# One slot for the values' sums, bf16 filler matmuls of 512 columns, and a new issue order in a sketched-attention and experts kernel

## The chip, the cores and the metric

The kernel runs on one core of a Trainium2 chip, in one launch. Times are device microseconds (us). The core's engines work side by side, each through its own list in order: PE does the matmuls (PEld is its loading of the stationary operand), DVE, ACT and POOL work on vectors, and SP issues most DMAs. In this kernel PE's results go to PSUM, from where DVE and ACT read them. A matmul of f32 operands shows in the trace as two weight loads and two matmul records; a transpose on PE shows as one of each.

## The reference

Two parts follow each other, for a batch of 4, 1088 positions and 4 heads of 32:

```
phi(x) = (S1 x) outer (S2 x)            # 8 x 8 features per position and head
kv = sum_s phi(k) v ;  z = sum_s phi(k)
x  = (phi(q) kv) / (phi(q) z + 1e-6)    # heads side by side: (4, 1088, 128)

logits = x w_gate ; the two largest of 4 experts, softmax weights over these two
for each expert e:  a = softmax(causal(scale (x wq_e)(x wk_e)^T))
                    out += weight_e * (a (x wv_e)) wo_e     # where e was chosen
```

## The kernel before

**Stages.** For each of the four batches b the kernel first makes x (`prepare`, L342): the sketches of k and q (`sketch`, L434), ACT copies of these (L444), features on DVE or POOL (L454), the sums kv (L489), transposed features (L503), numerators (L524), the division on DVE (L532 to L535), x transposed (L541) and the logits (L585). From the logits DVE chooses the experts (`choose`, L608 to L615). Positions are cut into 17 pieces of 64, and these into groups 0, 1 and 2 of 6, 6 and 5 pieces. For each group come the queries (`queries`, matmuls L707, picked by masks on DVE at L717), the scores of each piece (`scores`: matmul L749, DVE takes them at L754, exponential on ACT at L769, reciprocal on DVE at L774, scaling on POOL at L778, transpose on DVE at L783), the values' sums (`values`, L805), the reading of these sums (two copies by ACT at L829, two products at L839 and two predicated copies at L843 on DVE) and the output product (`outputs`, L863).

**PSUM.** Four single tiles `bank0` to `bank3` serve most matmuls (pool `ps`). One further tile, `V`, spans four banks (L137). Before the main work, batch 0 uses three of V's banks as slots of the pool `ps0` (L143), one bank each, for its sketches, sums, transposes, logits and masks. Later V holds the values' sums: a group writes columns 0 to 191 of all four banks, or columns 256 to 447, the two slots of the pool `V` (L144). The framework that builds the program makes an instruction wait for earlier accesses of the list that it takes to be in conflict with it.

**Batch 0's masks.** The masks of its group 0 do not go through memory: six products of a one-hot matrix with the choice (`widen_masks`, L636) spread them over the partitions, each into a slot of `ps0`, and ACT or DVE copies each out (L641). The query picks at L717 need these copies.

**Order.** The kernel collects 1320 jobs, each with its engine, the values that it reads, what it makes and the slots that it holds. `ORDER` (L68) is a list of job numbers, two letters each, written out beforehand; `Plan.run` (L34) issues the jobs in that order and hands a slot to the first job that names it and back after the last. So the list fixes each engine's order and also which access of a PSUM tile counts as the earlier one. The entry `--` is no job but calls `nothing` (L926): a matmul of zeros into the last 64 columns of V's fourth bank, which nobody reads. The list has 69 of them, all before the first values' sums. They stand in runs, called filler matmuls here: 39 before the first sketch, then 1, 10, 2, 1, 1, 3, 5, 1 and 6.

Decoded, PE's list up to the first scores runs as follows (sk: sketch of k or q, batch/half; kv: sums; tq: transposed features; wt, mp: products of weights; num, tx, lg: numerators, transposed x, logits of a third; qe: queries; sc: scores; a number times `--` is a run of filler matmuls):

```
39x-- sk/k/0/1 -- sk/k/0/0 10x-- sk/q/0/0 kv kv tq/1 tq/0 wt0 wt1 2x-- sk/q/0/1 -- mp/1 sk/k/1/0
num/0 sk/k/1/1 tq/2 tq/4 tx/0 -- tq/3 num/1 sk/q/1/1 sk/q/1/0 tx/1 num/2 lg/1 3x-- tx/2 mp/0 lg/2 lg/0
4 qe 5x-- 3 masks -- 3 masks 6x-- 3 tq of batch 1, qe, 3 sc, tq, sc, qe, kv of batch 1, qe, kv of batch 1, ...
```

Where the sums of two groups meet, PE's list has this many other PE jobs between the last block of the one group and the first of the next (batch,group): 0,0 to 0,1: 20; to 0,2: 14; to 1,0: 11; to 1,1: 16; to 1,2: 0; to 2,0: 41; to 2,1: 0; to 2,2: 20; to 3,1: 0; to 3,2: 3; to 3,0: 0. At the five with 0 or 3, some of the reads of the earlier group (L829, L839, L843) stand in the list after the first blocks of the next.

Of the kernel before, what the change touches and what calls it, by code (L numbers as in the profile page):

```python
# [10 lines left out]
BF16 = mybir.dt.bfloat16  # L11
# [7 lines left out]
class Plan:  # L19
# [10 lines left out]
    def job(self, eng, us, rank, f, reads=(), makes=None, holds=(), kb=0.0, wait=0.0):  # L30
        self.jobs.append(dict(eng=eng, us=us, rank=rank, f=f, reads=tuple(reads), makes=makes, holds=tuple(holds),
                              kb=kb, wait=wait, n=len(self.jobs)))
# [34 lines left out]


ORDER = """
AAACAEABADATASAUAQARAFAPAVAWALANAMAIAJAOAGAHAKAbAZ------------------------------------------------------------------  # L70
------------AhAjAi--AdAkAfAeAgAaAXFlAc--------------------AlAYAmAvFmAnAoAwA0FpAxAyFoA1B6FnAzB8FrB7FqB9----ApAqAr--CB
FsAuAsFuFwCDCCA8FxAtFyF2A9FzA2F4F3F0A6BAA+A3A7Ft--A4F1A/FvBFA5F5GDBGF9F6GFGEBHBJF/BOF8BIGGF+BZBPGABa------BQBSGIB+BR
BEBBBbGCB/BDCABXBcBMBvCGGHBKBLCJCHBNF7CIBCBYCEBwBdBWB1CFBxGBB2BT----------BkBiBqBVBeBlGJBjBzBf--BmBoB3BrBgBUBpBnBhCL
C2C7CK------------GRCNGNGSCMGVGODMBsB4GWCOCaCPCsCQCbGTCcCRCtCgGUCdDJChCuB5BtGLBuDKCvCSByCiCeCTDHCwCjCfGKDICkCxB0ClGM
DLDNEJEEDOCmDPEVDQEXEWCnKoDXEcEYKqCoEbDlKrDYDnKmDmDZCUCpEZDoCqCVDpEaDaEdKsDbGPCrKpCWEeDtKnDcGQDvCXDuGpCYDqDwDrEfCZDx
GqCyDyDsGtDzGgEgD0CzGhD1GrD2C0GkGsKvG2C1GiC9C6DRC3G3GjC+G0C4C8DdG1DfC5D3DeDSDBD4DTKwC/D5DUDgDVDAKuDhDWGXD6KtDCD7EpFT
DEGYFYDGEhDFDDD8GZGbEnGaEiGyDiEjEoDjFBGzEqFDEkE/ErDkElHHG4D9HID+EsFAG5EmEtD/G+FCG6HAEuEAHBG8HCFEFFEBECG/FGLEG7EGEIED
FHELE3G9LGEHLFExEMEKE4EvFIEFE5LHEwPnE6HFLJEyE7EOPoHLLKHDHKLIHGE8EPEzHME9HOKxE0IKE1KyE+KzIIILK0INE2IJENHEK1IOFJIPH3K2
EQIRH8K3ETESJYEUPuK5ERIMK4PwJZK6JWIQJaJXK8JcIYJdJeISK7IZI4ITIaK9IeLMIUIbIfIcIVK+IdIWLLPxK/LAIXLBHJPqLNPvPrJbLDHNPpI2
JfPtLCHnPsI3HVHoFKI5HpHWLSI6HqLUHrLWFLLTI7I8LVIgHXGfFMGeI9LXGcGdIhFNHYIiHZHhIjFOIkHiHjIlFPGoGmHkHlGlHPFQGnHQHRFRHSHT  # L80
LQGwHmFSPyGuFXFaFULRGvHaJwHUGxPzFbFZP0HsHtJxP1HbHuKCP3HcHvKAFVFWHdJyP2HwKBFcHeKDHxJzFeHfHyJ0HgFdFgJ1J2HzKZKUFfH0FjFk
FiH1FhIuH+H2H7JgH5H4IvIwH6H9JiIxH/KEIyJ3IAIBIzKFI0JhKGIoJjImI1JkICKHInKIIpJ6JKJlJFJ4JmKJIqLOIDJ5LPJoIEIrIHJ7IsLqIFJp
J8IGJqItLrI+J9JrLuJ+LsJnLhJsI/J/LtLiLYJAJtLlLZJuLjLcJvLaLkL3LbL1L4LzL2MGL0L5NJMHMLNKMIJBMJMBL6MCJCMDL7JDL9KKJHJEL/JJ
JMKLJIJNJGMEKML8MFJLL+KNLfMALeKOLdLgKPKQLpLmMMLoKRMNLnMPJPNLJONQNMNPMKNNMOJQNRMiOGMQOLMjNOMRJRKSMSJTNSOZLxMkMTKbMUNT
LvKWKYLwKcKTNZLyKaOaMVNUJSJVN3KVKXNVJUNaOXNWKdNbMlN4NXOdMmOYKfNYNcMnNdP4OeKhNeMuP5P6MWMvKeP7MXMwNnP9KgMxP/M9KlNoM4Kj
OcMyQAKkNpMYOgKiP+N5MzQBP8NqNvN6NrNxQCMZNwQMNyN7MaNsQEMbMoNzN8QNQDMpMqN0N1QFQOMrQPMsN2QGObQHNtQQQRMtMcOfQIQSNfNuQZN9
MdNgMeOhQaQKOjOiQbQdQLNhN+QcQJQ0OkPFQ1OlQXNiQVMfPBMgQYOmMhQWOnPDPCNjOxPEPGQTOyPHOzNkNlM0O0QUPINmPJO1QrQiQsM1QjQvQtOp
QuO2QmO3Q4OqQkOrQ5QlQ2OsRJQ3OtQ6M2N/RKM3M8M5OAPKQ7RCOoQ+OBM+RDRAO4REOCQ8M/M6ODOuM7NAOEQ/OvRBRFNCOIOFOKONQ9OHNDOJOOOM
NBOwRGO5PaPVSXNEO6NFRHSYNIO7NHRNRINGRORMO8SVRQO9OQSbORSWO+O/ScRLTnPATlToOPRPTmTrRXTsSESJRvOSRYRnOVRZOWRROTOURaRtRSRb
PLRuRTRcRlRwR1RURxRmRVPMRoR2RpRyRWPNRzRqRrRdR0QhRfQfReQgSZRsQeSaRgR3SdRhPOSeR4RiR5SfRjShSgS3RkSiS5R6SjS4R7PPS6SkS7R8  # L90
PQSlSvQqS8S9QpSxQnSwQoS/SyTBTASzTDTCTpTES0PRTFTtS1PSTGTHPTR9QwSmPZQzPUPbQxS+QyR+PWPcS2SnR/PdPXTISpSAPYSoSqPeSrSBSCSs
StPfSLSDSISuSFPgPhSKSMTqPiSGUcPkTJUXSHPjPmTuPlSOUHUNUISPUJUOUPUKSNULUQUMTvURSQT7TwTKTTSUUSTxSRT8STTYTyUBTzT9SST1TLT0
UCT2UDT+T/TMT3UEUAUFT4TNT5UGT6TOTPTQTRUTTVTSTXTaTUTWUUTbTZUVTcUZUbUWUeUdTdUaUfUYTeTfUhTgTkThUgTjTiUiUjUkUlUmUn
"""


# [1 line left out]
def kernel(  # L98
# [14 lines left out]
    nc = tc.nc  # L113
# [17 lines left out]
    def const(name, shape, dt=F32):  # L131
        return cp.tile(shape, dt, name=name, tag=name)

    def several(name, n, shape, dt=F32):
        return [const(f"{name}{x}", shape, dt) for x in range(n)]

    V = pp.tile([128, 4, 512], F32, tag="V", name="V")  # L137
    banks = [pp.tile([128, 512], F32, tag=f"bank{x}", name=f"bank{x}") for x in range(4)]
# [2 lines left out]
    pools = dict(  # L141
        ps=banks,
        ps0=[V[:, x] for x in range(3)],  # L143
        V=[V[:, :, 0:192], V[:, :, 256:448]],  # L144
        kin=several("kin", 1, [128, S]),
        qin=several("qin", 1, [128, S]),
        vp=several("vp", 1, [128, NJ, H, D + 1]),
# [16 lines left out]
        A=several("A", 4, [128, S]),  # L164
# [13 lines left out]

    idle = const("idle", [128, 128])
    SKW = const("SKW", [128, 2, 2, 2, R])
    ident = const("ident", [128, 128])
    mask = const("mask", [128, 512], BF16)
# [608 lines left out]
    def values(b, n, rank):  # L793
        t0, t1 = groups[n]
        nt = t1 - t0
        AT, Vk, agg, mb = ("AT", b, n), ("V", b, n), ("agg", b, n), ("mb", b, n)
        J = 2 * t1

        def block(j0, j1):
            a = plan[AT][:, 0 : J * nt * 32].rearrange("p (j t s) -> p j (t s)", t=nt, s=32)  # L800
            for j in range(j0, j1):
                lo = 32 * max(0, j // 2 - t0)
                for g in range(4):
                    rows = slice(32 * g, 32 * g + 32)
                    nc.tensor.matmul(plan[Vk][:, g, lo : 32 * nt], plan[(f"xr{j // 12}", b)][rows, j % 12], a[rows, j, lo:],  # L805
                                     start=(j == 0), stop=(j == J - 1))

        def cost(j0, j1):
            n = [32 * (nt - max(0, j // 2 - t0)) for j in range(j0, j1)]
            return sum(max(0.22, 2 * x / 1200 + (0.03 if x > 160 else 0.006)) for x in n)  # L810

        for j0 in range(0, J, 4):
            j1 = min(j0 + 4, J)
            xr = (f"xr{j0 // 12}", b)
            need = [("AT", b, n), ("xr", b, j0 // 12)] + before
            before[:] = [("V", b, n, j0)] if j1 < J else [("V", b, n)]
            job("PE", cost(j0, j1), rank + 0.001 * j0, lambda j0=j0, j1=j1: block(j0, j1), need, before[0], [AT, Vk, xr])
# [10 lines left out]
        def keep(x):  # L828
            nc.scalar.copy(halves(plan[uw][:, x, 0:w]), part(x))  # L829

        def widen(x):
            nc.scalar.copy(plan[agg][:, 3 * x, 0:w], plan[mb][:, 3 * x, 0:w])

        def outer(x):
            a = plan[agg][:, 3 * x, 0:w]
            nc.gpsimd.tensor_tensor(out=a, in0=a, in1=plan[uw][:, x, 0:w], op=ALU.mult)  # L836

        def inner(x):
            nc.vector.tensor_tensor(out=halves(plan[agg][:, 1 + x, 0:w]), in0=part(x),  # L839
                                    in1=halves(plan[mb][:, 1 + x, 0:w]), op=ALU.mult)  # L840

        def patch(x):
            nc.vector.copy_predicated(halves(plan[agg][:, 1 + x, 0:w]), halves(plan[mb][:, E + x, 0:w]), part(1 - x))  # L843

        r = rank + 0.1
        for x in range(2):
            job("ACT", w * 0.00084 + 0.05, r, lambda x=x: keep(x), [("V", b, n)], ("uw", b, n, x), [Vk, uw])
            job("ACT", w * 0.00094 + 0.05, r - 0.05, lambda x=x: widen(x), [("mb", b, n)], ("agw", b, n, x), [agg, mb])
            job("POOL", w * 0.0023 + 0.08, r, lambda x=x: outer(x), [("uw", b, n, x), ("agw", b, n, x)], ("agg", b, n), [uw, agg, mb])
            job("DVE", w * 0.00104 + 0.08, r, lambda x=x: inner(x), [("V", b, n)], ("agg0", b, n, x), [Vk, agg, mb])  # L850
            job("DVE", w * 0.00104 + 0.08, r, lambda x=x: patch(x), [("agg0", b, n, x)], ("agg", b, n), [Vk, agg, mb])
# [72 lines left out]
        if b + 1 < B:  # L924
            prepare(b + 1, lambda x, b=b: 100.0 * b - 15 + 90 * x)
    def nothing():  # L926
        nc.tensor.matmul(V[:, 3, 448:512], idle, idle[:, 0:64], start=True, stop=True)  # L927

    with tc.manual_schedule():
        plan.run(places(ORDER), nothing)  # L930
# [30 lines left out]
```

## Time and profile before

| what | us |
|---|---|
| three timed runs, median (lowest, highest) | 377.95 (376.8, 378.43) |
| the profiled execution | 376.98 |
| its span, first to last instruction | 374.9 |
| PE busy, of the span | 336.3 (90%) |
| DVE busy | 208.2 (56%) |
| POOL busy | 142.6 (38%) |
| ACT busy | 139.8 (37%) |
| PE busy on values' sums L805, scores L749, outputs L863 | 90.9, 78.3, 42.3 |
| PE busy on filler matmuls L927 | 30.6 |
| mean granted clock of PE | 0.937 |

The span has two parts. Up to about 88 us one batch's preparation runs by itself, and PE, ACT and DVE hand work to each other. From there to 368.5 us PE is busy nearly throughout, and 6.4 us of copying and storing the last outputs follow. The timeline's columns are start, length, engine, line, operation, result and operand, shape, count, and in brackets the idle time of that engine just before and what ended it. A merged row of a timeline stands for the number of records behind its x.

### The profile page before, as it was taken

To read this page: it belongs to the slowest core of one execution; us is meant where nothing else is said; L and a number is where in the kernel's file an instruction comes from. 1 tells how busy PE (TensorE), PEld (TensorE's weight loads), DVE (VectorE), ACT (ScalarE), POOL (GpSimd) and SP (SyncE) were. 2 spreads that over 40 slices of the span, in tenths; PEclk is the share of its full clock that TensorE was granted. 3 is DMA by queue.
4 is the path that set the end of the run, shared out by engine and by line. 5 is a ranking of instruction groups with operands and counts; after the bars stand their busy time and mean duration, and the time that the engine had idled before them with its cause. 6 is when DMAs were issued, how large, how long until landed. Compare 5 with 4: busy or idle time off the path is not lost.

```text
span 374.9 us, 11451 instructions
## 1 busy us (share of the span) xinstructions
PE 336.3 (90%) x4812; PEld 263.0 (70%) x4812; DVE 208.2 (56%) x626; ACT 139.8 (37%) x401; POOL 142.6 (38%) x235
## 2 busy tenths in 40 slices
PE   8988676779999989999999789999969999999783
PEld 8987575467667757687757687675667676768782
DVE  6042022513798978756498324778754687575230
ACT  1000232214545437454472203786403554234101
POOL 5100076150233496736342410795172133431220
PEclk9999997665999999999999969999997999999968
DMA  7604302930570164188002228300121043301001
GB/s 170 126 10 69 45 23 76 171 93 1 76 124 24 44 137 80 37 126 158 19 15 69 65 57 157 83 17 21 42 67 35 21 94 72 91 4 32 11 0 38
DMA packets 79039, 24.39 MB, mean 65 GB/s; under 512 B 51084, under 2 KB 77964, under 8 KB 78988
## 3 DMA queue, kind: packets, MB, share of 16 engines
q1 hardware_dynamic: 78972, 23.66, 31.0%
q8 instruction: 37, 0.61, 0.7%
q14 instruction: 14, 0.11, 0.1%
q10 hardware_dynamic: 16, 0.00, 0.0%
HBM read 19.18 MB, written 4.48 MB: 63 GB/s over the span
## 4 chain that ended last, share of the span: by engine, by line
PE 76%; DVE 12%; ACT 8%; issue 2%; POOL 1%; DVEq 0%; ACTq 0%
PE V L805 21%; PE bank L749 14%; PE bank L863 9%; PE V L927 8%; PE bank L707 7%; DVE A L754 2%; PE V L434 2%; DVE agg L843 2%; PE bank L524 2%; DVE agg L839 2%; PE bank L489 2%; PE bank L503 2%; ACT uw L829 2%; PE V L636 2%; ACT A L769 2%
## 5 line engine op out<-in xcount | busy, mean ns | idle before, releaser
L778 POOL TENSOR_SCALAR A<-A,rs,sh 128x64 f32<-128x64 f32 (+14 forms) x68 | 55.7, 822 | 104.2 <-DVE rs L774 103.6
L749 PE MATMUL bank<-xT,qs 128*128 128x384 f32 (+10 forms) x216 | 78.3, 487 | 1.0 <-ACT ob L871 0.7
L769 ACT ACTIVATE A<-A,mx 128x64 f32<-128x64 f32 (+13 forms) x68 | 52.6, 774 | 58.7 <-DVE mx L754 55.6
L805 PE MATMUL V<-AT,xra 32*128 32x192 f32 (+5 forms) x1152 | 51.1, 321 | 8.7 <-DVE agg L843 4.2
L805 PEld LDWEIGHTS V<-AT,xra 32*128 32x128 f32 x1152 | 44.1, 195 | 16.8 <-issue 6.0
L783 DVE STREAM_TRANSPOSE AT<-A 128x64 f32<-128x64 f32 (+14 forms) x68 | 51.4, 765 | 4.7 <-POOL A L778 4.4
L749 PEld LDWEIGHTS bank<-xT,qs 128*128 128x128 f32 x216 | 37.1, 192 | 22.6 <-issue 8.4
L863 PEld LDWEIGHTS bank<-Mo,agg 128*128 128x128 f32 (+1 forms) x288 | 39.0, 206 | 7.2 <-issue 2.3
L863 PE MATMUL bank<-Mo,agg 128*128 128x128 f32 (+1 forms) x288 | 42.3, 302 | 1.1 <-DVE mx L754 0.6
L754 DVE CUSTOM_DVE_ANT_0 A<-bank,mask 128x384 f32<-128x384 f32 (+11 forms) x68 | 33.9, 509 | 16.6 <-PE bank L749 15.9
L927 PE MATMUL V<-idle 128*128 128x64 f32 x138 | 30.6, 411 | 9.6 <-ACT mb L641 3.3
L707 PE MATMUL bank<-xT,Mq 128*128 128x384 f32 (+1 forms) x96 | 37.7, 510 | 1.4 <-DVE mx L754 0.7
L927 PEld LDWEIGHTS V<-idle 128*128 128x128 f32 x138 | 29.0, 318 | 12.1 <-ACT mb L641 4.1
L836 POOL TENSOR_TENSOR agg<-agg,uw 128x384 f32<-128x384 f32 (+1 forms) x24 | 22.6, 954 | 32.0 <-ACT uw L829 31.4
L717 DVE COPY_PREDICATED qs<-mb,bank 128x384 f32<-128x384 uint8 (+1 forms) x48 | 25.1, 551 | 14.8 <-PE bank L707 11.4
L805 PEld LDWEIGHTS V<-AT,xrb 32*128 32x128 f32 x768 | 27.6, 196 | 6.3 <-issue 2.6
L805 PE MATMUL V<-AT,xrb 32*128 32x160 f32 (+5 forms) x768 | 29.5, 302 | 2.4 <-DVE agg L839 1.2
L454 POOL TENSOR_TENSOR fp<-qab 128x512 f32<-128x512 f32 (+1 forms) x18 | 17.0, 968 | 34.7 <-ACT qab L444 34.6
L839 DVE TENSOR_TENSOR agg<-V,mb 128x384 f32<-128x384 f32 (+1 forms) x24 | 12.6, 532 | 27.5 <-PE V L805 20.5
L707 PEld LDWEIGHTS bank<-xT,Mq 128*128 128x128 f32 x96 | 17.2, 201 | 12.5 <-issue 3.1
L754 DVE CUSTOM_DVE_ANT_0 A<-bank,mask,mx 128x320 f32<-128x320 f32 (+7 forms) x40 | 24.2, 610 | 2.3 <-PE bank L749 1.2
L829 ACT COPY uw<-V 128x384 f32<-128x384 f32 (+1 forms) x24 | 10.1, 464 | 34.7 <-DVE agg L839 29.8
(133 smaller groups left out, 387.1 us busy)
## 6 DMA issues: line engine op xcount, KB each, us to landing
xra<-xd SPq DMA_DIRECT2D x16, 192.0 KB
xrb<-xd SPq DMA_DIRECT2D x16, 192.0 KB
xrc<-xd SPq DMA_DIRECT2D x16, 160.0 KB
qin<-in_q_dram SPq DMA_DIRECT2D x16, 136.0 KB
mb<-md SPq DMA_DIRECT2D x7, 288.0 KB
kin<-in_k_dram SPq DMA_DIRECT2D x12, 136.0 KB
vp<-in_v_dram SPq DMA_DIRECT2D x12, 128.0 KB
xd<-xs SPq DMA_DIRECT2D x8, 192.0 KB
```

Source lines behind the costliest of these rows:

```text
L707: nc.tensor.matmul(plan[t][:, 0:w].rearrange("p (h t s) -> p h t s", h=2, s=32), Mq[:, e], xv, start=True, stop=True)
L717: nc.vector.copy_predicated(mine(l), halves(plan[mb][:, c, 0:w]), halves(plan[t][:, 0:w]))
L749: nc.tensor.matmul(plan[p][:, 0 : c1 - c0], plan[qs][:, 128 * t : 128 * t + 128], plan[xT][:, c0:c1], start=True, stop=True)
L754: nc.vector.tensor_tensor_reduce(out=plan[A][:, c0:c1], in0=plan[p][:, 0:w], in1=msk, scale=-1.0, scalar=mx[:, b, i, x - 1 : x] if x else ...
L769: nc.scalar.activation(out=a, in_=a, func=ACTF.Exp, bias=mx[:, b, i, last : last + 1], scale=-1.0, accum_out=zs[:, b, i : i + 1])
L778: nc.gpsimd.tensor_scalar(out=a, in0=a, scalar1=rs[:, b, i : i + 1], scalar2=plan[("sh", b)][:, i : i + 1], op0=ALU.mult, op1=ALU.mult)
L783: nc.vector.transpose(dst[:, 0 : keys // 32, t], plan[A][:, 0:keys].rearrange("p (j s) -> p j s", s=32))
L805: nc.tensor.matmul(plan[Vk][:, g, lo : 32 * nt], plan[(f"xr{j // 12}", b)][rows, j % 12], a[rows, j, lo:], start=(j == 0), stop=(j == J - 1))
L836: nc.gpsimd.tensor_tensor(out=a, in0=a, in1=plan[uw][:, x, 0:w], op=ALU.mult)
L839: nc.vector.tensor_tensor(out=halves(plan[agg][:, 1 + x, 0:w]), in0=part(x), in1=halves(plan[mb][:, 1 + x, 0:w]), op=ALU.mult)
L863: nc.tensor.matmul(plan[p][0:m, 128 * x : 128 * x + 128], plan[agg][:, e, 128 * x : 128 * x + m], Mo[:, e], start=(e == 0), stop=(e == E - 1))
L927: nc.tensor.matmul(V[:, 3, 448:512], idle, idle[:, 0:64], start=True, stop=True)
```

## The change

Three edits. The pool `V` gets one slot, columns 0 to 191. The filler matmul becomes one bf16 matmul of 128 x 128 by 512 columns into the whole fourth bank of V (the operand `idle` is bf16 and four times as wide). And `ORDER` is another permutation of the same 1320 jobs with 65 filler matmuls.

```diff
 ORDER = """
-AAACAEABADATASAUAQARAFAPAVAWALANAMAIAJAOAGAHAKAbAZ-----...
+AAACAEASADATAUABAQARAPAVAWANAFAOAKAMALAZAHAJAGAIAb-----...
...
@@ pools
-        V=[V[:, :, 0:192], V[:, :, 256:448]],
+        V=[V[:, :, 0:192]],
@@
-    idle = const("idle", [128, 128])
+    idle = const("idle", [128, 512], BF16)
@@
     def nothing():
-        nc.tensor.matmul(V[:, 3, 448:512], idle, idle[:, 0:64], start=True, stop=True)
+        nc.tensor.matmul(V[:, 3], idle[:, 0:128], idle, start=True, stop=True)
```

The new list, decoded in the same way:

```
42x-- sk/k/0/0 -- sk/k/0/1 3x-- sk/q/0/0 -- sk/q/0/1 kv tq/0 tq/1 kv wt0 tq/3 tq/2 wt1 tq/4 2x-- num/1
sk/k/1/0 sk/k/1/1 -- num/2 tx/1 2x-- lg/1 tx/2 sk/q/1/0 num/0 sk/q/1/1 lg/2 tx/0 mp/0 kv of batch 1, 3 qe
mp/1 kv of batch 1, lg/0 qe 6x-- 3 masks -- 3 masks 6x-- 4 tq of batch 1, 4 sc, 3 qe, sc, ...
```

In the list of all engines: on SP, one of the two loads of the sketch matrices moves behind three loads of v, and the stores and fetches of x and of the masks of batch 0 are mixed otherwise. On DVE, one of the transposes of k now stands between the decoding of the sketch matrices and its spreading and the transposes of q stand between the two feature products of k. On PE, the logits of group 0 of batch 0 come after three of its query products. On POOL, the weights of the choice stand further ahead among batch 1's features.

Other PE jobs between two groups' sums, in the new list: 0,0 to 0,1: 14; to 0,2: 19; to 1,0: 5; to 1,1: 15; to 1,2: 5; to 2,0: 17; to 2,1: 19; to 2,2: 20; to 3,1: 13; to 3,2: 12; to 3,0: 0. With one slot, all six reads of a group stand before the first block of the next.

More of the change, by code (lines that the diff above doesn't have):

```diff
@@ L69 @@
 ORDER = """
[L70 to L93, printed above, removed]
+AAACAEASADATAUABAQARAPAVAWANAFAOAKAMALAZAHAJAGAIAb------------------------------------------------------------------
@@ new lines @@
+------------------AdAeAf--AhAgAaAiAjAc------AlAYFlAXAkAnAm--ApFmAoAvArAqAtAyA0AsAzAwA1AuB6FpAxA4FnB7A2FoA5B8FqA3A6Fr
+B9A7----BFFsFuFwBGF2FxFyFzF4--BOBJF3F1BHBPBIF5----BZFtBSBQF0BaBRF9FvA8F6F+F/GDA9F7BbGEGFBcA+BAF8BvB+A/GAGKGGB/CABKBw
+CGBMB1CEBxGBCHB2CIBWCFB3BUCBBTBLGLCDBNCCBzBXGMBVCJBCBYGCBdBEByBBGJBDGIB4------------BeBmBoBfBpBn--BiBqBgBjB5BkBrGHBh
+BlCKBsC2C7CL------------GPCMGRGQB0CNGVGSGTGWCmGUCaCnCsCbCoBtCOCtDHBuCcCpCPDJCqCQCdDMCeCrDICRDKCfCgCSDOEJEEChDLCuDQCU
+CTEZDNCiCvEVDPCwCjDlCVEWCkCxCWDnDmKoClD1KqDoCXKpDdDpD2CYKnD3DeDqCZEXDrD4CyEcD5KsDsKmCzEYD6D7EbDvEdKrC0D8DXC4C1C6C9C3
@@ new lines @@
+DRC5DtDYC8DSEaDZDuDfEeDTGNDaDgDbDwGODUDhC+GXDVDcC/DxDWGYDADyDBDiGbKwDzKvEfDjDCFYDDEvD0FTDEDFEhDkDGEnKtEgD9EoEiGgEwEj
+KuGpGhD+EkGqGkElGiGZGjGrGtEmGaG0GsGyG1G2GzHHG3G4FDHILED/LGLFLHFBE/G5EALJG8FAFCG6LKEBFELIG+FFK+HAECLAFGK/FHK3G9ELEIED
+EGExG7K5EKEMK4HFFIHBG/EFE3HGEyHCE4EpEzEHE5EqE0EPErE6EOE1HDE7EsHLHKHMEtE2KxPnK6ENKyEuKzHEJWH8K9HOJYPoH3K8E8JXHJEQJdJZ
+JaE9HNETIIJcERJeESHnK7IJE+EUHbHtK0HoFJLBHcHpHuFKK1HdHqHvHeHrHhPwIMHfK2IKHsHgFLHiILLDIPHjIOLLGeHkLCIQGdPuGcLMGfHlHwPx
+HxLQPtLNHmLOPqHyLRFMPrPvLPPpFNPsHVLYHWHXHPLZFOHYFPHQGlHZHRGoHaGnFQHSHTGmLcHUFRLaGuFVFSLSGxFXFaFUINLbGvFWLTGwLzFbFZIR
@@ new lines @@
+LhL0HzLiImLlLjInIoLkI2IpISIqI3IuITL1IrIUIvIsFdL2IVItI4IWFeIXI5IgFgI6IYIeIZH0I7IaIfI8IhJbIiIbIwJfIcLUI9LWLVH1IdLXLqIj
+IxH2IkH+H7KAIyLrH4FcH9KBLuLsH/JFKCLtIlJiFfJKKDFkL3FhH5JgFiL4FjH6KEJhIBKFJjKGICIzL5I0JqJkIAKHJoJlL6I1IDKUIGPyJmKZJpIH
+I+IEPzJrKIL7P0JnJsL/J4P1KJL9JwMBP2IFMCJtMIJ5J6JxMDMJL8JyJ7MAMKJ8JzL+MGNLJ0J9JuMEI/MFNMJvJ+MHJAMNP3MMNJJ/NNNKMOJBJ1J2
+NPJCNQNRJDJ3QFJJJMJEJLOcJHQHOXJNQGJGJIMLOYNOQIMPKKNSQKNfNhQJNgKLNiQLNjMQMoMRNkMSJQNlMpMTMqMUJONmMrMiMsJPMjMkMWKMOLMX
+MlOGMmJRKNLfMYJSJUMZKOMaJVLeLdKPJTLgKQLnLmLoOZLpKROeOaOdKSOgP/LyMVKTMbLvKYMnMuKVQALxMtQBMcLwKbKaNnMvN3MdQCMwNoN5KcMe
@@ new lines @@
+QDMxN4P4MfN6ObMyP5KWNpN7MgKXMzQEKfMhP6NqKeP7N8NrOfQPN9KhNsQRQQQVP8N+QSKdQWP+QTM9NtOxKgM4KiP9M0QUNuKkKjOyKlQNQMNvQOQi
+NwQZQjM1QaQmM2QdQbM/M3NTM8M6M5QcQXNANZQYM7M+NUQrNaNVNCQsNbNDNWQvNcNXQtNBNdNYQuNeQ4NENxPVQ5NFPaOpNINyNHNzPBNGOqQ0PCOr
+Q1N0QkN1OsPFQlPDOtN2Q2PEN/OuPGOvQ3PHQ6OAOBOwQ7OCRCQ+PIPJRDRAODREQ8PKOEO7OFOIOKONO5Q/OJOOOzRBOHO6RHQ9O0OMOhRFRIO8O1RJ
+RGOiOQO9O2O3OPRORKORO+O4O/OjOSRNSEOURMPASJOVSVOTOWRLOkSWRQOlSXRPSZScR3SYOmOnSbR1SdRlR2RROoRnRmPLR4RoR5RtRSRvRuRpPMR6
+RwR7RTRqPNRrR8RxPOQgRURsRVQhQfRyRdRWRzQeRXReR0PPRYPQRZPRQqRaRbQnQoPSRcQpPTRfQyPcPUTnQwPZPXPWQzPdSaQxToPYPbTlRgSeRhTp
@@ L94 @@
+TrS3TtTmRiTsS5RjS4TBRkS/S6TDTAS7SpTCTESnS8TFS9SxSoR9SqS+SrPeTGSsTHSvR+StTISuR/SwSASySzSBSCS0S1SfSGSDSISLPgSFSgPfS2SK
+PiShSHUXSMUcTqPhSiSOPmTuSjPjPlUHPkSNSkUISlUJSPSmTvSQUNUKTYTwSRULT7TxSSUOTJSUTTUMUPSTTyT8TzT1TKT9UQT0T2URT3T+TLT/UST4
+UAT5TMT6TNUBTOUCUDTPUEUFTQUGTRTaTXTSTVTZTbTWTUUTUUUVTdUeUWUbUZUYTcUfUaUdTeTfUgTgTkTjUhTiThUiUjUkUnUmUl
 """
```

## The prediction

> **What bounds the kernel now.** I read the page first (PE busy 90% of the span; the chain of work that ended last is 76% PE, and 8% of it is the filler matmuls of L927), then PE's timeline, which falls into two parts.
>
> Up to 88 us it is a relay. The lines of PE's timeline that carry this:
>
> ```profile
> 1.07 16.91 PE L927 MATMUL V<-idle 128*128 128x64 f32 x78 [1.07 <-DVE A L210]
> 17.90 2.42 PE L434 MATMUL V<-SKW,kT 64*64 64x32 f32 x80
> ...
> 24.07 4.53 PE L927 MATMUL V<-idle 128*128 128x64 f32 x20 [0.54 <-ACT kab L444]
> 28.53 1.99 PE L434 MATMUL V<-SKW,qT 64*64 64x32 f32 x64
> ...
> 48.93 1.45 PE L524 MATMUL V<-kvz,fp 64*64 64x33 f32 x48
> ...
> 55.39 0.90 PE L524 MATMUL V<-kvz,fp 64*64 64x33 f32 x48 [0.57 <-ACT xT L545]
> ...
> 72.73 1.22 PE L927 MATMUL V<-idle 128*128 128x64 f32 x10
> ```
>
> Two things are to be seen. First, the 39 fillers at the start are themselves the wait: DVE's timeline has the sketch matrix spread by 7.4 and both transposes of k done by 8.9 us, and PE comes to the sketch at 17.9. Second, one filler record takes 16.91 / 78 = 0.217 us here and 1.22 / 10 = 0.12 at 72.7, and the numerators 1.45 and then 0.90. The table of windows prints a granted clock of 1.00 for both, but up to about 50 us PE runs like the stretches that it prints as 0.50 (the fillers at 85 us: 12 in 2.82). So 17 us of f32 fillers did not lift the clock, nor did the 4.5 us at 24.
>
> Every use of V is also strung in list order there. ACT's second copy of q's sketch waits for the sums listed before it, which lie in another bank:
>
> ```profile
> 30.58 0.27 ACT L444 COPY qab<-V 128x128 f32<-128x128 f32 x1 [6.56 <-PE V L434]
> 33.16 0.27 ACT L444 COPY qab<-V 128x128 f32<-128x128 f32 x1 [2.32 <-PE V L489]
> ```
>
> So the slots of V are not independent, and this carries over to the second part, where PE is busy except at the joints between two groups' sums:
>
> ```profile
> 210.98 1.35 PE L805 MATMUL V<-AT,xra 32*128 32x160 f32 x32
> 214.50 2.16 PE L805 MATMUL V<-AT,xra 32*128 32x160 f32 x32 [2.16 <-DVE agg L839]
> 217.81 2.52 PE L805 MATMUL V<-AT,xra 32*128 32x160 f32 x32 [1.15 <-DVE agg L843]
> ```
>
> The next group's first block waits for reads of the previous sums, a later read waits for that block, and the next block for that read, though the columns differ. The idle time lowers the clock: the windows give 0.73 for 214 to 216, 0.50 to 220, 1.00 from 222. The same 32 records take 1.35 us before and 2.2 to 2.5 after.
>
> **The dense part, step by step.** From the first batch 1 transposes (87.97) to PE's end (368.5) it takes 280.5 us.
> - Joints. PE's idle rows with L839, L843 or L829 behind them between 200 and 340 us are 2.16, 1.15, 0.98, 1.21, 1.17, 0.87 and 0.45: 8.0 us. They lie at joints with 0 or 3 PE jobs between. The new list has 5 to 20 at all joints but the last, and joints with 11 or more now show no wait. Those with 5 have some 3 us of PE work against the reads: ACT 2 x 0.48 beside DVE 2 x 0.55 + 2 x 0.58, 2.3 us if nothing is queued ahead. I leave 1 us for each: +2.0. The last joint (2.44 and 0.62 us at 356) stays, as nothing stands in it.
> - The clock after them. 215.5 to 220.9 and 279.9 to 286.6 run at half clock. In the first, 2.16 and 2.52 us stand against 1.35 each, and the rest makes it 2.4; in the second, 24 output records take 5.23 us against 2.84 at 118 us, and a block 1.93 against about 1.2: 3.2. Gone: -5.6.
> - kv of batch 1 moves ahead of this part: 2 x 1.2 = -2.4 (paid below).
> - 88 to 92 us is at half clock; with the masks' part at full clock -1.9.
>
> 280.5 + 2.0 - 8.0 - 5.6 - 2.4 - 1.9 = 264.6. Other jobs of the list keep their number and form; where their order differs I take nothing, with +-4 for waits on DVE, which is 86% busy from 108 to 150 us (36.3 of 42). That cover is thin: a read of V late on DVE now stops every later sum.
>
> **The relay, step by step.** No row shows a bf16 matmul. Above, its price is an f32 record of the same 512 columns (L749, 12.2 us / 24 = 0.51, less the 0.1 that a line through 320 and 512 columns leaves at none: 0.41); below, half of that, 0.21, for half the bytes; the same slope gives 0.42 at half clock for the lower one. I take 0.21 at full clock, because of the two ends it is the nearer to the one warm row of this operation itself (0.12 for a 64-column record), and keep both.
>
> The Trainium skill (TensorE: Matmul & The Clock Gate, Part 1) has 215.7 ns for a warm bf16 matmul of 512 columns and 426.7 for a cold one. It also says that about 3.4 us of sustained matmuls lift the clock, whatever they are; the row at 1.07 speaks against the last part. By the rule taken literally, the old fillers had already warmed PE, the new ones would change only their own price, and the relay would gain 8 us at its head and little behind it.
>
> - Start. In the rows a lift came some 3.5 us after dense work resumed (217.8 to 220.9, 88 to 92). So 42 fillers: 8 cold in 3.4 us, 34 x 0.21 = 7.1; the sketch starts at 1.07 + 10.5 = 11.6 instead of 17.9. Behind this cover lies SP's move: one sketch matrix is issued after three loads of v (3 x 0.43), so the decoding starts 1.3 to 2 us later than 2.37; with its 4.7 us, the transpose of k (0.7) and the spreading (0.4) it is ready at 9.5 to 10.5. Without the fillers this would set the start.
> - To the first numerators (now 17.9 to 48.9, 31.0 us). Strung along the new list: four sketches 2.0, 2.4, 2.0, 2.4, sums 2 x 2.14, transposes 4 x 1.1 and 0.7, weights 1.1 and 0.7, ten hand-overs of 0.3 to 0.7 by ACT and 7 fillers come to 29.8 cold. At full clock the same rows from later batches (sums 1.2, four transposes 0.6, sketches at most 60%) make it 20. PE would be busy about two thirds of it, as at 50 to 60 us, where the clock held. I take 25.
> - To the masks (now 48.9 to 74.8, 25.9 us, some of it at full clock). With kv of batch 1 inside: 20.7 if all is warm, 31.5 if all is cold. I take 25.
> - Masks to batch 1 (now 13.1; one half of the masks took 2.21 us and the other 4.21 at half clock, and 18 filler records): 8.3 to 12.5. I take 10.
>
> The dense part starts at 11.6 + 25 + 25 + 10 = 71.6 (bounds 60.6 and, cold throughout with fillers at 0.41, 92). DMAs do not hold it: the new list's last fetches of x and masks on SP are issued by some 55 to 65 us (18 x 0.47 us after the last store of x) and read after 72. POOL's batch 1 features (6.4 us for k, 6.5 for q, the choice 5.8) end before the masks do.
>
> **Sum.** 71.6 + 264.6 + 6.4 (last copies and stores) = 342.6 span; the profiled execution has 376.98 - 374.9 = 2.1 around it: **344.7**. That execution is 0.3% below the median of the runs shown, so I say 345.
>
> **Rivals.**
> - The fillers neither warm PE nor cost less: start 1.07 + 42 x 0.41 = 18.3, then 29.8 + 27 + 12.5, and the cold start of the dense part stays: 87.6 + 266.5 + 8.5 = 363. For: no kind of filler has lifted the clock yet. Against: the 64-column ones are mostly weight loads (PEld is busy 16.8 of the 16.9 us).
> - The joints' waits come back in another place, because the reads are queued on DVE: relay as forecast, dense 280.5 - 2.4 - 1.9 = 276.2: 356.
> - Slower: the single slot stops PE at the joints. A full wait is the reads' 2.3 to 3.3 us and then some 2.5 at half clock, 5.5 in all; 0 PE jobs between gave such. The relay and the removed waits are worth 34 us together, so from 7 of the 11 joints on it is slower; 8 give 71.6 + (280.5 - 4.3 - 13.6 + 44) + 8.5 = 387. Against: 5 to 20 jobs stand there.
> - Neither part does what it says: 87.6 + 278.1 + 8.5 = 374.
> - All warm, no new wait: 60.6 + 262.6 + 8.5 = 332.
>
> **Chances.** Forecast (338 to 354) 0.55, joints elsewhere 0.15, fillers useless 0.12, all warm 0.08, neither 0.05, slower 0.05. The range 336 to 364 leaves out the last two, most of the all-warm case and the tails. About 0.5% can be told from no change here: faster 0.92 (all of the first four and part of "neither"), within 0.03, slower 0.05.
>
> **What would show it.** Filler records of 0.2 us from about 5 us on, the first sketch at 11 to 12 us, the numerators' 48 records in 0.9 rather than 1.45 us, the first batch 1 transposes near 72, no idle over 1 us at joints but the last, no stretch at 0.50 between 100 and 340. Wrong if fillers stay at 0.42, if PE falls back to cold rates within the relay, or if DVE rows with L754 or L783 stand ahead of the reads at a joint.

## The result and the profile after

The changed kernel takes 345.08 us (median of 4 runs, 341.02 to 346.73) against 377.9 (376.8 to 378.43): ratio 0.910, 95% interval 0.901 to 0.918. Forecast were 345. Its executions lie up to 6 us apart, the longer ones with a lower mean clock (0.961 in the shortest, 0.935 in the longest), and the one profiled here is the longest, with 346.73 us and a span of 345.0, so that its relay is late; the two-slot kernel below has the same list and fillers and was profiled in a shorter one.

PE's timeline of the changed kernel, at the places shown of before (start, length, instruction, count, idle time before and what ended it):

```profile
1.21 11.99 PE L927 MATMUL V<-idle 128*128 128x512 bf16 x42 [1.21 <-DVE A L210]
13.13 1.20 PE L434 MATMUL V<-SKW,kT 64*64 64x32 f32 x64
...
28.05 1.08 PE L503 MATMUL V<-ident,fp 128*128 128x128 f32 x4 [0.40 <-ACT kvz L496]
...
35.45 1.51 PE L524 MATMUL V<-kvz,fp 64*64 64x33 f32 x48
...
64.39 2.21 PE L636 MATMUL V<-cT,AT 64*128 64x192 f32 x12 [1.28 <-DVE g L615]
...
77.53 2.39 PE L503 MATMUL bank<-ident,fp 128*128 128x128 f32 x14
```

The fillers end 4.8 us earlier, and behind them a sketch of 64 records takes 1.20 us where it took 1.99: the clock is up. It does not stay up. At 28 us four transposes take 1.08, and the numerators at 35.45 take their cold 1.51. The first transposes of batch 1 start at 77.53 instead of 87.97. (In the two-slot kernel's profile, whose list is the same, four of these transposes at 28.57 still take 0.63, and batch 1 starts at 70.78.)

PE's longest waits in the changed kernel (engine, line, what it waited for: total, times, longest):

```profile
PE V L805 <- DVE agg L843: 2.7, 1, 2.7
PE V L927 <- ACT mb L641: 2.6, 2, 1.7
PE V L927 <- ACT xT L545: 1.8, 1, 1.8
```

Of the waits of the sums for reads, one is left. It is the last joint, first before and then after:

```profile
356.57 1.15 PE L805 MATMUL V<-AT,xra 32*128 32x128 f32 x32 [2.44 <-DVE agg L843]
358.34 1.93 PE L805 MATMUL V<-AT,xra 32*128 32x64 f32 x32 [0.62 <-DVE agg L843]
360.20 8.24 PE L863 MATMUL bank<-Mo,agg 128*128 128x128 f32 x48
```

```profile
322.74 2.43 PE L805 MATMUL V<-AT,xrc 32*128 32x160 f32 x80
327.90 4.71 PE L805 MATMUL V<-AT,xra 32*128 32x192 f32 x96 [2.74 <-DVE agg L843]
332.54 5.99 PE L863 MATMUL bank<-Mo,agg 128*128 128x128 f32 x48
```

The dense part as one window, from the first transposes of batch 1 to PE's end, first before and then after (busy times of PE, PEld, DVE, ACT and POOL, then the granted clock):

```profile
87.97:368.50 280.53, 265.12 (x3921) 200.83 (x3920) 181.60 (x543) 122.44 (x350) 114.94 (x166) 0.96 0.29 60
```

```profile
77.53:338.53 261.00, 251.87 (x3850) 188.94 (x3848) 180.89 (x543) 121.37 (x348) 114.88 (x166) 0.99 0.26 58
```

It is 19.5 us shorter: PE's idle time in it fell from 15.4 to 9.1 us, and its busy time by 13.2, of which 2.4 are the sums of batch 1 that moved ahead of it. The other 10.8 us go with the clock, whose mean rose from 0.96 to 0.99: the other matmuls are the same. So of 30 us of span in this execution, 10.4 come from the relay and 19.5 from the dense part; against the two-slot kernel's profile, 36 us shorter than before, it is 17.2 and 18.8.

### The profile page after: what moved, and what is told of

Its sections match the earlier page's. It is cut to its first block, busy times and chain, and to the rows that moved or that the text cites. A ratio compares the mean times of both kernels' runs of the same rounds, so it can differ in the third digit from the quotient of the medians.

```text
span 345.0 us, 11306 instructions
## 1 busy us (share of the span) xinstructions
PE 313.2 (91%) x4739; PEld 228.1 (66%) x4739; DVE 206.5 (60%) x626; ACT 138.9 (40%) x401; POOL 142.4 (41%) x235
## 4 chain that ended last, share of the span: by engine, by line
PE 77%; DVE 14%; ACT 5%; issue 2%; POOL 0%; DVEq 0%; ACTq 0%
PE V L805 22%; PE bank L749 16%; PE bank L863 8%; PE bank L707 8%; PE V L927 6%; DVE A L754 3%; DVE agg L839 2%; PE bank L489 2%; PE V L636 2%; ACT uw L829 2%; PE bank L434 2%; DVE AT L783 2%; PE bank L524 2%; PE bank L503 2%; DVE agg L843 2%
## 5 line engine op out<-in xcount | busy, mean ns | idle before, releaser
L778 POOL TENSOR_SCALAR A<-A,rs,sh 128x320 f32<-128x320 f32 (+15 forms) x68 | 55.8, 823 | 95.5 <-DVE rs L774 88.1
L749 PE MATMUL bank<-xT,qs 128*128 128x384 f32 (+11 forms) x216 | 79.6, 486 | 1.8 <-DVE mx L754 1.3
L769 ACT ACTIVATE A<-A,mx 128x320 f32<-128x320 f32 (+15 forms) x68 | 52.5, 772 | 58.6 <-DVE mx L754 55.4
L783 DVE STREAM_TRANSPOSE AT<-A 128x320 f32<-128x320 f32 (+15 forms) x68 | 50.9, 763 | 9.6 <-POOL A L778 9.1
L805 PE MATMUL V<-AT,xra 32*128 32x192 f32 (+5 forms) x1152 | 48.8, 314 | 3.3 <-DVE agg L843 2.7
L805 PEld LDWEIGHTS V<-AT,xra 32*128 32x128 f32 x1152 | 43.0, 191 | 12.2 <-issue 5.8
L863 PEld LDWEIGHTS bank<-Mo,agg 128*128 128x128 f32 (+1 forms) x288 | 34.1, 185 | 6.6 <-issue 2.9
L863 PE MATMUL bank<-Mo,agg 128*128 128x128 f32 (+1 forms) x288 | 37.2, 280 | 0.6 <-DVE mx L754 0.6
L836 POOL TENSOR_TENSOR agg<-agg,uw 128x384 f32<-128x384 f32 (+1 forms) x24 | 22.5, 954 | 32.6 <-ACT uw L829 32.3
L927 PE MATMUL V<-idle 128*128 128x512 bf16 x65 | 20.9, 473 | 8.1 <-ACT mb L641 2.6
L805 PEld LDWEIGHTS V<-AT,xrb 32*128 32x128 f32 x768 | 25.9, 185 | 2.5 <-issue 2.3
L805 PE MATMUL V<-AT,xrb 32*128 32x160 f32 (+5 forms) x768 | 27.5, 290 | 0.0
L707 PEld LDWEIGHTS bank<-xT,Mq 128*128 128x128 f32 x96 | 17.2, 198 | 15.6 <-DVE mx L754 3.9
L839 DVE TENSOR_TENSOR agg<-V,mb 128x384 f32<-128x384 f32 (+1 forms) x24 | 12.8, 531 | 18.6 <-ACT uw L829 9.6
L829 ACT COPY uw<-V 128x384 f32<-128x384 f32 (+1 forms) x24 | 10.2, 463 | 32.5 <-DVE agg L839 26.3
L454 POOL TENSOR_TENSOR fp<-qab 128x512 f32<-128x512 f32 (+1 forms) x18 | 17.1, 968 | 11.1 <-ACT qab L444 11.0
L774 DVE RECIPROCAL rs<-rs 128x1 f32<-128x1 f32 x68 | 10.1, 151 | 13.8 <-ACT rs L771 13.7
```

Of the source, the lines that this page charges most:

```text
L707: nc.tensor.matmul(plan[t][:, 0:w].rearrange("p (h t s) -> p h t s", h=2, s=32), Mq[:, e], xv, start=True, stop=True)
L749: nc.tensor.matmul(plan[p][:, 0 : c1 - c0], plan[qs][:, 128 * t : 128 * t + 128], plan[xT][:, c0:c1], start=True, stop=True)
L769: nc.scalar.activation(out=a, in_=a, func=ACTF.Exp, bias=mx[:, b, i, last : last + 1], scale=-1.0, accum_out=zs[:, b, i : i + 1])
L778: nc.gpsimd.tensor_scalar(out=a, in0=a, scalar1=rs[:, b, i : i + 1], scalar2=plan[("sh", b)][:, i : i + 1], op0=ALU.mult, op1=ALU.mult)
L783: nc.vector.transpose(dst[:, 0 : keys // 32, t], plan[A][:, 0:keys].rearrange("p (j s) -> p j s", s=32))
L863: nc.tensor.matmul(plan[p][0:m, 128 * x : 128 * x + 128], plan[agg][:, e, 128 * x : 128 * x + m], Mo[:, e], start=(e == 0), stop=(e == E - 1))
```

## The experiments

**The new filler alone** (old list, two slots):

```diff
-    idle = const("idle", [128, 128])
+    idle = const("idle", [128, 512], BF16)
-        nc.tensor.matmul(V[:, 3, 448:512], idle, idle[:, 0:64], start=True, stop=True)
+        nc.tensor.matmul(V[:, 3], idle[:, 0:128], idle, start=True, stop=True)
```

> The kernel before with the new filler matmul alone (one bf16 matmul of 512 columns in place of the f32 one of 64); old list, two slots. Theory: the fillers carry part of the gain by their price and by lifting the clock, the list the rest. 39 head fillers end at about 12.5 us instead of 17.9, the two sketches behind them run in 1.2 and 1.45 instead of 2.0 and 2.4 us, the run of ten in 2.1 to 4.3 instead of 4.5, the dense part keeps its 280 us and its idle times at the joints: 366 to 370 us. Rival, the list does everything: 376 to 378. Rival, the fillers do most of it: under 355.

Measured: 356.94 us, ratio 0.948 (0.941 to 0.954), twice the expected gain. PE's timeline of this kernel:

```profile
1.20 10.63 PE L927 MATMUL V<-idle 128*128 128x512 bf16 x39 [1.20 <-DVE A L210]
...
15.83 2.32 PE L927 MATMUL V<-idle 128*128 128x512 bf16 x10 [0.54 <-ACT kab L444]
18.08 1.20 PE L434 MATMUL V<-SKW,qT 64*64 64x32 f32 x64
...
31.93 0.90 PE L524 MATMUL V<-kvz,fp 64*64 64x33 f32 x48
...
69.90 1.42 PE L503 MATMUL bank<-ident,fp 128*128 128x128 f32 x10
...
194.99 1.37 PE L805 MATMUL V<-AT,xra 32*128 32x160 f32 x32 [2.16 <-DVE agg L839]
197.53 2.52 PE L805 MATMUL V<-AT,xra 32*128 32x160 f32 x32 [1.17 <-DVE agg L843]
```

The dense part starts at 69.9 us, 18 earlier than before and about as early as under the new list in the two-slot kernel (70.78); here the clock stayed up to the numerators (0.90 us), 13.9 us behind the start of q's sketch at 18.08; before it was 20.4 (28.53 to 48.93). The joints at 195 are as they were. So the relay's gain needs no new list.

**The new list and slot alone** (old filler):

```diff
-    idle = const("idle", [128, 512], BF16)
+    idle = const("idle", [128, 128])
-        nc.tensor.matmul(V[:, 3], idle[:, 0:128], idle, start=True, stop=True)
+        nc.tensor.matmul(V[:, 3, 448:512], idle, idle[:, 0:64], start=True, stop=True)
```

> The changed kernel with the old f32 filler of 64 columns; new list, one slot. Theory: 42 head fillers at 0.434 end at 19.3 us instead of 13.1, and the sketches, sums and transposes up to 27 us run cold again (5 to 6 us); the dense part stays at 260 to 262 us: 355 to 359 us. Rival, the list does everything: 343 to 347. Rival, the fillers do most of it: over 365.

Measured: 362.73 us, ratio 0.962 (0.957 to 0.966), above the expected range. In the profiled execution, which took 368.08 us, the dense part starts at 94.6 us and takes 265.3, against 280.5 before. So the list's gain lies in the dense part. That its relay is longer under the old fillers is not shown: the start is 6.6 us later than before, but the other three executions are 4 to 7 us shorter than this one. The two ratios multiply to 0.911, the whole change: filler and list add up.

**Two slots with the new list.**

```diff
-        V=[V[:, :, 0:192]],
+        V=[V[:, :, 0:192], V[:, :, 256:448]],
```

> The changed kernel with the two slots of before; new list and new filler. Theory: all reads of a group stand ahead of the next group's blocks in the list, and the slots were never independent, so nothing changes: within 1% of the changed kernel's 341 to 347 us, no new idle time at the joints. Rival, the single slot itself matters, for good or ill: over 2% apart.

Measured: 344.08 us, ratio to before 0.912 (0.906 to 0.917). The slot by itself does nothing: what the list brings, it brings with two slots too. In the profiled execution (340.66 us) the first sketch starts at 12.36, the dense part at 70.8, and it takes 261.7. PE's timeline:

```profile
28.57 0.63 PE L503 MATMUL V<-ident,fp 128*128 128x128 f32 x4 [0.77 <-ACT AT L328]
...
32.84 1.51 PE L524 MATMUL V<-kvz,fp 64*64 64x33 f32 x48
...
70.78 3.04 PE L503 MATMUL bank<-ident,fp 128*128 128x128 f32 x14
```

Here the clock holds for some 5 us longer than in the changed kernel's profile, but the numerators are cold in both. The masks start at 57.64.

**Reads of the sums taken off V**, in the kernel before and in the changed one. The six instructions of a group at L829, L839 and L843 read a constant in SBUF, so the output lacks the values' sums.

```diff
         def part(x):
-            return plan[Vk][:, 2 * x : 2 * x + 2, 0 : 32 * nt]
+            return Mq.rearrange("p e d -> p (e d)")[:, 0:384].rearrange("p (h s) -> p h s", h=2)[:, :, 0 : 32 * nt]
```

> The kernel before, in which the six reads of each group's sums (L829, L839, L843) take columns of a constant in SBUF in place of V, so that nothing of V's sums is read; the number and size of the instructions stay. Theory: the dense part of before loses about 19 us at the joints, by waits (8.0 us between 200 and 340, 3.1 at the last joint) and by the half clock behind them (5.6 and about 3): 357 to 361 us, and dense 261 to 264 us without a stretch at 0.50. Rival, the joints' waits are made up elsewhere and the new list's other changes give the dense part its gain: over 371.

> The changed kernel with the same reads taken off V. Theory: only the last joint still costs (2.7 us and a half-clock stretch of 3): 337 to 341 us, 1 to 1.5% under the changed kernel. Rival, the single slot holds up PE or the clock in other places too: under 334.

Measured: 353.33 us from the kernel before (ratio 0.937, 0.934 to 0.941) and 335.26 from the changed one (0.891, 0.884 to 0.897). Both fell more than expected, the first by 24 us, the second by 10; the second lies between its expected range and that of its rival. The dense part of the first, as a window:

```profile
87.75:344.50 256.75, 253.52 (x3922) 192.23 (x3922) 187.47 (x543) 122.17 (x349) 123.90 (x166) 0.99 0.31 65
```

With the old list and the old fillers the dense part falls from 280.5 to 256.8 us as soon as the sums need not wait for reads: 12.2 us of idle time and 11.6 of busy time, clock 0.99 instead of 0.96. (The reads no longer wait for the sums either; but of PE's idle time before, L805's waits for the three reads alone were 11.1 us: 5.4 for L843, 3.8 for L839 and 1.9 for L829.) So the joints carry the dense part's gain, in two nearly equal halves, waits and clock. The changed kernel keeps some of it: taken off V there, 261 to 262 becomes 254.3.

**Narrow fillers**, three bf16 matmuls of 64 columns in place of one of 512:

```diff
-        nc.tensor.matmul(V[:, 3], idle[:, 0:128], idle, start=True, stop=True)
+        for _ in range(3):
+            nc.tensor.matmul(V[:, 3, 0:64], idle[:, 0:128], idle[:, 0:64], start=True, stop=True)
```

> The changed kernel with each filler as three bf16 matmuls of 64 columns instead of one of 512. Theory: the clock follows the share of time in which columns stream, and a 64-column matmul is mostly weight load, bf16 or not; the clock is not lifted at the head, the first sketch of 64 records takes 2.0 us and not 1.2: 349 to 357 us, depending on how long the head lasts. Rival, it was the f32 type that kept PE cold, and any dense bf16 stream lifts the clock: the first sketch takes 1.2 us, 341 to 347 us.

**f32 fillers of 256 columns**, 20 at the head:

```diff
-    idle = const("idle", [128, 512], BF16)
+    idle = const("idle", [128, 256])
-        nc.tensor.matmul(V[:, 3], idle[:, 0:128], idle, start=True, stop=True)
+        nc.tensor.matmul(V[:, 3, 0:256], idle[:, 0:128], idle, start=True, stop=True)
```

> The changed kernel with f32 fillers of 256 columns, 20 instead of 42 at the head; one look for the clock. Theory that the share of time in which columns stream decides: with 256 columns a record is mostly stream, so the clock rises during the head and the first sketch of 64 records takes 1.2 us. Rival, f32 matmuls do not lift the clock whatever their width: 2.0 us. The time itself tells little, as a filler of this kind lasts longer.

Measured: 341.89 us (338.81 to 347.11) with the narrow ones, and 350.71 in one run with the f32 ones. PE's timeline of the narrow ones and then of the f32 ones:

```profile
1.20 6.27 PE L928 MATMUL V<-idle 128*128 128x64 bf16 x126 [1.20 <-DVE A L210]
8.95 1.33 PE L434 MATMUL V<-SKW,kT 64*64 64x32 f32 x64 [1.47 <-DVE SKW L296]
```

```profile
1.20 11.88 PE L927 MATMUL V<-idle 128*128 128x256 f32 x40 [1.20 <-DVE A L210]
13.02 1.20 PE L434 MATMUL V<-SKW,kT 64*64 64x32 f32 x64
```

Both lifted the clock, so neither "64 columns are too few" nor "f32 does not count" holds. What my expectation for the narrow ones missed is the price: such a bf16 record takes about 43 ns in the cold stretch (23 or 24 a microsecond from 2 to 6 us, 30 in the one after) where the f32 one took 217, so its 64 columns come five times as often, though PEld is busy all the time there too (1.00 of each microsecond from 2 to 7). The f32 stream with four times the columns lifts the clock and the one with 64 does not; that fits the share of time in which columns stream, though no run isolates this share. The rival with the type falls.

**A short head**: 20 fillers at the head, and the sketch matrix's load back at the front of SP's list (the first line of the list whole, the next cut):

```diff
-AAACAEASADATAUABAQARAPAVAWANAFAOAKAMALAZAHAJAGAIAb------------------------------------------------------------------
-------------------AdAeAf--AhAgAaAiAjAc
...
+AAACAEABASADATAUAQARAPAVAWANAFAOAKAMALAZAHAJAGAIAb----------------------------------------AdAeAf--AhAgAaAiAjAc------
...
```

> The changed kernel with 20 fillers at the head instead of 42, and the first sketch matrix's load back at the front of SP's list. Theory: the head then ends with the sketch matrix, near 8 us instead of 13.1, and the clock is lifted by then (it rose at 6.5), so the time falls by about 5 us: 336 to 341. Rival, the longer head pays for itself by holding the clock further into the relay: no gain, 341 to 347.

Measured: 341.48 us (340.43 to 342.57), ratio 0.906 (0.902 to 0.909). The sketch starts at 9.4 us, 3.7 earlier than in the changed kernel, held by the sketch matrix; the dense part starts at 72.8. At most 3.6 us (345.08 to 341.48) remain of it, less than expected and, by the two intervals, not clear of none: the relay behind it is cold from its transposes at 26.47 us on (1.09 us for four), and its numerators, at 32.03, take 1.51.

**No filler at all**,

the same list without its 65 `--`. Of it the first line:

```diff
-AAACAEASADATAUABAQARAPAVAWANAFAOAKAMALAZAHAJAGAIAb------------------------------------------------------------------
...
+AAACAEASADATAUABAQARAPAVAWANAFAOAKAMALAZAHAJAGAIAbAdAeAfAhAgAaAiAjAcAlAYFlAXAkAnAmApFmAoAvArAqAtAyA0AsAzAwA1AuB6FpAx
...
```

> The changed kernel without any filler. Theory: the first sketch starts with the sketch matrix at 9 us, and the whole relay runs cold (numerators 1.45 us, masks 4.2 each half): the dense part starts 77 to 84 us, 345 to 353 us, so that the new fillers are worth up to 8 us and the old ones cost more than none. Rival, the relay does not hang on the clock: the head's 4 us are gained, 337 to 342.

Measured: 343.6 us (342.07 to 344.27), ratio 0.911 (0.908 to 0.914). PE's timeline of this kernel, whose line numbers are one lower (L433 for L434):

```profile
8.96 2.13 PE L433 MATMUL V<-SKW,kT 64*64 64x32 f32 x64 [8.96 <-DVE SKW L295]
...
35.71 1.51 PE L523 MATMUL V<-kvz,fp 64*64 64x33 f32 x48 [0.74 <-ACT fp L506]
...
74.14 3.17 PE L502 MATMUL bank<-ident,fp 128*128 128x128 f32 x14 [1.28 <-DVE qs L716]
```

The time is just under the expected range and above the rival's. The sketch starts 4.2 us earlier than in the changed kernel and runs cold (2.13). At the numerators this kernel is level with the changed kernel's profile (35.71 against 35.45) and behind the two-slot kernel (32.84); its dense part starts at 74.14, between 77.53 and 70.78. So the new fillers pay back about what they cost: without them the changed kernel takes the same time within the spread. And with the old ones it takes 362.73, some 19 us more than with none. Most of what the change gained in the relay is thus the cost of the old fillers. No run has the old list without fillers; there the new fillers took 20 us off (377 to 356.94).

**The old list's relay ahead of the new list's dense part**: the old list up to the first transposes of batch 1, then the remaining jobs in the new order. Of it the first line:

```diff
-AAACAEASADATAUABAQARAPAVAWANAFAOAKAMALAZAHAJAGAIAb------------------------------------------------------------------
...
+AAACAEABADATASAUAQARAFAPAVAWALANAMAIAJAOAGAHAKAbAZ------------------------------------------------------------------
...
```

> The changed kernel with the old list up to the first transposes of batch 1 and the new list's order for all jobs behind; new fillers, one slot. Theory after the first runs: the new list gains in the dense part alone, and the old list's relay is no worse under new fillers (dense start 69.9 us in the filler-only kernel, 71 to 78 in the changed one): dense start near 70, dense part 263 with the sums of batch 1 in it, 339 to 345 us. Rival, the new list's relay is worth several us as well: over 348.

Measured: 341.9 us (340.43 to 344.68), ratio 0.908 (0.903 to 0.913); dense start 71.3, dense part 261.1 with 2.7 us for the sums of batch 1 in it. The new order of the relay is worth nothing; the new order of the dense part is all of the list's gain.

**V as two tiles** of two banks, list and fillers as changed:

```diff
-    V = pp.tile([128, 4, 512], F32, tag="V", name="V")
+    V = [pp.tile([128, 2, 512], F32, tag=f"V{x}", name=f"V{x}") for x in range(2)]
-        ps0=[V[:, x] for x in range(3)],
-        V=[V[:, :, 0:192]],
+        ps0=[V[0][:, 0], V[0][:, 1], V[1][:, 0]],
+        V=[[v[:, :, 0:192] for v in V]],
-                    nc.tensor.matmul(plan[Vk][:, g, lo : 32 * nt], ...
+                    nc.tensor.matmul(plan[Vk][g // 2][:, g % 2, lo : 32 * nt], ...
-            return plan[Vk][:, 2 * x : 2 * x + 2, 0 : 32 * nt]
+            return plan[Vk][x][:, :, 0 : 32 * nt]
-        nc.tensor.matmul(V[:, 3], idle[:, 0:128], idle, start=True, stop=True)
+        nc.tensor.matmul(V[1][:, 1], idle[:, 0:128], idle, start=True, stop=True)
```

> The changed kernel with V as two tiles of two banks instead of one of four; list and fillers unchanged, each sum's columns in the same banks. Theory that uses of V are strung in list order because they name one tile: hand-overs of the relay that touch different tiles overlap, the fillers wait for fewer reads, and at the last joint the first half of each block starts after half of the reads: 2 to 6 us less than the changed kernel, 336 to 342. Rival, the strings come from the banks or from the data: no change, 341 to 347.

Measured: 328.5 us (326.61 to 333.93), ratio to before 0.869 (0.865 to 0.873): below both kernels, and beyond the expected range. PE's timeline of it:

```profile
12.85 1.20 PE L434 MATMUL V<-SKW,kT 64*64 64x32 f32 x64
13.97 0.39 PE L927 MATMUL V<-idle 128*128 128x512 bf16 x1
14.29 1.67 PE L434 MATMUL V<-SKW,kT 64*64 64x32 f32 x80
...
28.82 0.90 PE L524 MATMUL V<-kvz,fp 64*64 64x33 f32 x48
```

The filler and the next sketch no longer wait for ACT's copy of the previous sketch (0.54 us idle at 14.86 in the changed kernel, none here). The numerators come 16.0 us after the first sketch instead of 22.3 (20.5 in the two-slot kernel), still warm; the dense part starts at 63.75 us and takes 256.8. No column lies in another bank than before. So the strings in V come from its being one tile, as the relay's lines of before suggested, and that was left in the change.

**Two tiles and more fillers**: the short head, and fillers (47, not the 43 of the expectation) where PE waits in the relay. Of the list, the second line of the new one, with its fillers between the jobs:

```diff
...
+AlAYFlAXAkAnAm--ApFmAoAv----ArAqAtAyA0------AsAzAw------A1AuB6----FpAxA4------FnB7A2------FoA5B8------FqA3A6------Fr
...
```

> As the kernel with two tiles, with 20 fillers at the head and the sketch matrix's load first, and with 43 more fillers put into the relay where PE waits for ACT or DVE. Theory: the relay's length hangs on the clock, and fillers in its gaps keep it up: the numerators' 48 records run in 0.9 us and both halves of the masks in 2.2, the dense part starts at 60 to 66 us, 328 to 335 us. Rival, the fillers fill the gaps but lengthen the chain by as much: 336 to 345.

Measured: 330.46 us (329.05 to 332.39), ratio 0.877 (0.872 to 0.882): inside the expected range, but no gain over two tiles alone (328.5), whose interval it just touches. PE's timeline of the profiled execution (332.39 us), whose line numbers are one higher (L435 for L434):

```profile
8.19 1.19 PE L435 MATMUL V<-SKW,kT 64*64 64x32 f32 x64
...
21.86 1.97 PE L490 MATMUL V<-vp,fp 128*64 128x33 f32 x36
...
30.73 0.90 PE L525 MATMUL V<-kvz,fp 64*64 64x33 f32 x48
```

The clock's mean is the highest of all profiles (0.980), but the dense part starts at 65.97, later than without them: the sketch starts at 8.19, the numerators only 22.5 us behind it, and the sums at 21.86 are cold all the same (1.97 us against 1.24). So the rival is right in kind though not in its range: fillers lengthen the chain by about what the clock gives. The shorter head and the load's place changed along with the fillers, and no run parts the three.

## Why the prediction was right, and where it was not

**The time** was right, 345 for 345.08, and the cases that carried it, joints and relay, are both in the profile. That it fits to a tenth is luck: the executions lie between 341.02 and 346.73, and errors of the terms cancelled. Against the profiled 346.73 the start of the dense part was put 5.9 us too early and the part itself 3.6 too long; against the two-slot kernel's 340.66 the start was 0.8 too late and the part 2.9 too long.

**Joints: right.** The 8.0 us of waits are gone, and no idle time of L805 that a read ended is left but the last joint's 2.74 us. With reads off V the old list loses 12.2 us of idle time in the dense part. The +2.0 for the two joints with five jobs between was not needed: L805 shows no wait there. Idle time in the dense part fell by 6.3 us against 6.0 forecast (8.0 less 2.0).

**The clock behind them: right in kind, too small.** The terms 5.6 and 1.9 were 7.5 us; measured are 10.8. I had counted the two half-clock stretches in the middle and the one at the start, but not the one at the end: before, the last joint had two waits, and the last outputs took 8.24 us for 48 records; after, one wait and 5.99. That is 2.3 us of the 3.3 that were missing; the rest was not traced.

**Start: right in kind.** 11.6 forecast, 13.13 measured: the clock came up near 6.5 us, after 5.3 us of fillers and not 3.4, so 13 fillers were cold and not 8. Prices were 0.43 and 0.21, as taken. The moment is not fixed: the 42 fillers take 11.23 us in the two-slot kernel's profile, and the 39 of the kernel with the old relay 9.95, in which by these prices some 8 were cold. At half clock a new filler costs what an old one cost (0.434), so all of the head's gain comes through the clock.

**The relay behind it: the failed step.** Its terms were 25, 25 and 10 us. Measured were 22.3, 28.9 and 13.1 in the changed kernel's profile and 20.5, 24.8 and 13.1 in the two-slot kernel's: 64.4 and 58.4 for 60, the first term too long in both and the last too short. The step that failed is the clock. I had let it hold up to the numerators, on the pattern of 50 to 60 us, where PE was two thirds busy, and had named a fall to cold rates within the relay as a sign of being wrong. It fell: at 27 us in the one, with PE busy 55% of the 3 us ahead, some 5 us later in the other, and the first numerators took 1.51 us in both, not 0.9. The last term is what it was before, 13.1, as the clock fell again there: its mean from the masks to batch 1 is 0.59 in the two-slot kernel, and the six fillers at its end take 2.72 us.

Nor does the new list, along which I strung the hand-overs, have a part in the relay's gain: the old list with new fillers starts the dense part at 69.9, and the old relay ahead of the new dense part gives the same time, 341.9 us.

**The fillers' worth: not seen.** The forecast took the fillers to earn their time. Without any, the time is the same. Under the new list the old ones cost 19 us and the new ones nothing on balance; the relay's gain is mostly a loss that was taken away. Nor did I try as a case that fillers might go.

**The rivals.** "Neither warm PE nor cost less" fell with the first sketch's 1.20 us. "The joints' waits come back" and "the single slot stops PE" fell with the waits' table, and "neither part" (374 us) with the time. The all-warm case, 332 us, was not reached by this change; V as two tiles went below it.

## What to carry to other kernels

When a matmul waits for a read of other columns of its tile, look first at whether the tile can be cut: here cutting one PSUM tile into two gave another 16 us, with every column in the bank it was in. A wait of PE can cost about twice its length where the clock falls behind it (here 12.2 us of waits and 11.6 of slower matmuls), so count both. And take filler work out once before tuning it: here, under the new list, the old fillers cost 19 us.

## What the runs showed of the hardware

- The clock column prints 1.00 from the start of a trace until the first fall or rise, also where the records run at half rate: the kernel before to about 50 us (0.217 us per filler record, 0.12 when warm), the kernel without fillers at its sketches (2.13 us against 1.20).
- 17 us of back-to-back f32 matmuls of 64 columns did not lift the clock; bf16 ones of 512 lifted it after 5.3 us in the changed kernel (an estimated 3.4 in the one with the old relay, from 39 fillers in 9.95 us at 0.43 and 0.21), bf16 ones of 64 near 6 us of the trace, f32 ones of 256 before 13. The Trainium skill (TensorE: Matmul & The Clock Gate, Part 1) ties the lift to some 3.4 us of sustained matmul activity; these traces agree in size for the bf16 streams, and the f32 one of 64 columns shows that matmul records end to end are not enough.
- A cold bf16 matmul of 512 columns takes 0.43 us and a warm one 0.21.
